# Who waits for the last two stores: moving one final wait from ScalarE to SyncE

## The chip, the cores and the metric

One core of one Trainium2 chip. The metric is device microseconds of one execution. The kernel takes about 98.8 us; its executions scatter by some 0.3 us.

## The reference, cut to what matters

One decoded token passes through attention over a window of 4096 keys and, in parallel, through an MLP. The result is one row of 1024 bfloat16 values.

```python
def reference(A_x, A_k_cache, A_v_cache, A_wq, A_wo, B_x, B_w1, B_b1, B_w2, B_b2):
    ...
    x = A_x                                       # 1 x 1 x 1024
    xn = _layernorm(x, axis=-1)
    return x + _A_ref(xn, A_k_cache, A_v_cache, A_wq, A_wo) + _B_ref(xn, B_w1, B_b1, B_w2, B_b2)
```

## The kernel before

Some 40 MB of weights and cache are loaded while the engines work behind the loads. The change touches only the end. TensorE collects the result in two halves of 512 columns, `ACC[0]` and `ACC[1]`. ScalarE copies the first half and SyncE stores it; VectorE copies the second and ScalarE stores that. Each storing engine then waits until its own store has landed.

```python
    with nc.body("pe_last", valid_engines=TENSOR):
        ...
        last.then_inc(s_fin, 1)
    ...
    dve.wait_ge(s_fin, 1)
    d_out = DVE.mark(dve.tensor_copy(OUT[32:33, :], ACC[1]))
    act.wait_ge(s_fin, 1)
    a_out = ACT.mark(act.activation(out=OUT[0:1, :], in_=ACC[0], func=ACTF.Copy))
    sp.wait_ge(ACT.sem, a_out)
    sp.dma_start(out_row[:, 0:512], OUT[0:1, :]).then_inc(s_out[0], 16)
    act.wait_ge(DVE.sem, d_out)
    act.dma_start(out_row[:, 512:1024], OUT[32:33, :]).then_inc(s_out[1], 16)
    sp.wait_ge(s_out[0], 16)
    act.wait_ge(s_out[1], 16)
```

Of the kernel before, what the change touches and what calls it, by code (L numbers as in the profile page):

```python
# [47 lines left out]
def bass_parallel_sum__sliding_block_cached__mixer_channel_mlp__decode_kernel(  # L48
# [21 lines left out]
    pe, dve, act, pool, sp = nc.tensor, nc.vector, nc.scalar, nc.gpsimd, nc.sync  # L70
# [12 lines left out]
    s_out = [nc.alloc_semaphore(f"s_out{n}") for n in range(2)]  # L83
# [490 lines left out]
    sp.dma_start(out_row[:, 0:512], OUT[0:1, :]).then_inc(s_out[0], 16)  # L574
    act.wait_ge(DVE.sem, d_out)
    act.dma_start(out_row[:, 512:1024], OUT[32:33, :]).then_inc(s_out[1], 16)
    sp.wait_ge(s_out[0], 16)
    act.wait_ge(s_out[1], 16)

    return nc  # L580

# [27 lines left out]
```

## Time and profile before

| | before |
|---|---|
| time, median of 3 runs | 98.78 us (98.54 to 98.88) |
| profiled run: time and span | 98.74 and 97.345 us |
| last matmul's semaphore to the end of the span | 1.977 us |

The span runs from the first to the last instruction that the profile records. The time is 1.4 us longer. No view shows it, but the trace's semaphore records go on past the span.

- **End**: the end of the span, which is the end of the last wait.
- **First barrier**: the nine steps of one semaphore that the kernel never names, counted in ns from the end. They are read as a barrier, in which each engine reports that it has arrived. A hop is the time from one step to the next; the turn is the hop from the fifth to the sixth. In the kernel before:

```
109  147  191  214  312  351  385  432     (the first of nine came at -1815)
```

- **Remainder**: time less span, averaged over the runs of a comparison. Spans are recorded to 0.1 us, so one run's remainder is coarse.

The rows of the profile that matter are shown in the prediction.

### The profile page before, as it was taken

What the parts mean: (1) busy time and instruction counts of PE and PEld (TensorE: products, weight loads), DVE (VectorE), ACT (ScalarE), POOL (GpSimd) and SP (SyncE); (2) the same over time, 40 slices, a digit from 0 to 9 for tenths busy, and PEclk for the clock granted to TensorE, in tenths of its full rate; (3) what the DMA queues carried; (4) which work ended last, traced back from release to release, by engine and by line L of the source; (5) the groups of instructions that cost most, each with busy time, mean ns of one, the idle gap of its engine ahead of it and who ended that gap; (6) DMA issues with size and microseconds to landing.
All of it is one profiled execution on the core that took longest, in us unless ns stands there. A gap on an engine that the chain in (4) does not pass through costs nothing.

```text
span 97.3 us, 1050 instructions
## 1 busy us (share of the span) xinstructions
PE 69.0 (71%) x330; PEld 32.3 (33%) x330; DVE 36.0 (37%) x49; ACT 5.8 (6%) x11; POOL 7.1 (7%) x23
## 2 busy tenths in 40 slices
PE   0001299999992139998999982169994699897881
PEld 0001154455550025655654431023341234332210
DVE  3705530000006999800999616794004300000002
ACT  0500060000000200000000000500000000000002
POOL 6796000000000000000000000000000000000000
PEclk9999999999999655999999999955699759999999
DMA  7999999989999989979999998888994999999970
GB/s 215 431 433 432 432 431 431 431 343 428 495 401 507 412 377 459 483 327 424 428 428 428 424 693 377 377 377 377 542 589 202 404 429 467 394 447 394 407 303 8
DMA packets 2773, 39.88 MB, mean 410 GB/s; under 512 B 322, under 2 KB 340, under 8 KB 724
## 3 DMA queue, kind: packets, MB, share of 16 engines
q1 hardware_dynamic: 2738, 39.85, 96.2%
q8 instruction: 1, 0.02, 0.1%
q10 hardware_dynamic: 34, 0.01, 0.1%
HBM read 39.86 MB, written 0.00 MB: 409 GB/s over the span
## 4 chain that ended last, share of the span: by engine, by line
DMA 79%; PE 15%; SPq 3%; issue 1%; DVE 1%; POOLq 0%
DMA W<-in_B_w_dram 42%; DMA KV<-in_A_wo_dram 37%; PE PS L404 7%; PE PS L388 7%; SPq L427 1%; SPq L169 1%; DVE KV L570 1%; SPq L179 0%; PE PS L560 0%; SPq L163 0%; POOLq L261 0%
## 5 line engine op out<-in xcount | busy, mean ns | idle before, releaser
L345 DVE STREAM_TRANSPOSE KV<-KV 128x4096 bf16<-128x4096 bf16 x4 | 17.5, 4424 | 5.3 <-DMA KV<-in_A_k_cache_dram 5.3
L388 PE MATMUL PS<-W,YZ 128*97 x64 | 14.7, 387 | 4.2 <-POOLq L261 4.1
L336 PE MATMUL PS<-WA,PT 128*97 x64 | 16.9, 434 | 0.2 <-issue 0.2
L388 PEld LDWEIGHTS PS<-W,YZ 128*97 x64 | 8.7, 136 | 10.2 <-issue 7.4
L336 PEld LDWEIGHTS PS<-WA,PT 128*97 x64 | 9.1, 142 | 7.7 <-issue 3.2
L505 PE MATMUL PS<-KV,PT 128*32 128x512 bf16 x32 | 9.8, 478 | 0.1
L538 PE MATMUL PS<-WA,GT 128*1 128x512 bf16 x56 | 7.9, 452 | 0.0
L570 DVE CAST KV<-PS 1x512 bf16<-1x512 f32 x1 | 0.7, 684 | 18.6 <-PE PS L560 18.6
L551 PE MATMUL PS<-W,OP 128*1 128x512 bf16 x48 | 6.8, 378 | 0.9 <-DMA W<-in_A_wo_dram 0.9
L296 PE MATMUL PS<-XT,meanf 128*128 128x16 f32 x2 | 0.6, 386 | 9.4 <-DVE XT L292 9.4
L348 DVE STREAM_TRANSPOSE TT<-PS 128x1024 f32<-128x1024 f32 x1 | 1.3, 1251 | 15.8 <-PE PS L336 15.8
L404 PE MATMUL PS<-KV,LQ 128*128 x32 | 7.1, 379 | 0.0
L505 PEld LDWEIGHTS PS<-KV,PT 128*32 128x32 bf16 x32 | 3.6, 116 | 5.8 <-issue 3.8
L404 PEld LDWEIGHTS PS<-KV,LQ 128*128 x32 | 3.1, 98 | 3.9 <-issue 0.6
L538 PEld LDWEIGHTS PS<-WA,GT 128*1 128x1 bf16 x56 | 2.7, 96 | 4.7 <-issue 2.3
L551 PEld LDWEIGHTS PS<-W,OP 128*1 128x1 bf16 x48 | 2.4, 83 | 5.3 <-DMA W<-in_A_wo_dram 1.2
L296 PEld LDWEIGHTS PS<-XT,meanf 128*128 128x128 f32 x2 | 0.5, 312 | 9.4 <-DVE XT L292 9.4
L510 DVE TENSOR_TENSOR TT<-PS,RM 32x512 f32<-32x512 f32 x1 | 0.7, 679 | 7.0 <-PE PS L505 7.0
L452 ACT ACTIVATE Pe<-PS,NMB 128x512 bf16<-128x512 f32 x2 | 1.3, 683 | 28.7 <-DVE NMB L449 28.7
L206 DVE MEMSET PS<- 128x3072 f32 x1 | 2.6, 2618 | 0.6 <-issue 0.6
L551 PE MATMUL PS<-KV,OP 128*1 128x512 bf16 x14 | 2.0, 378 | 0.6 <-DMA KV<-in_A_wo_dram 0.6
L431 DVE TENSOR_REDUCE MXP<-PS 128x1 f32<-128x1024 f32 x1 | 1.2, 1225 | 3.0 <-PE PS L404 3.0
(87 smaller groups left out, 30.1 us busy)
## 6 DMA issues: line engine op xcount, KB each, us to landing
WA<-in_A_wq_dram SPq DMA_DIRECT2D x2, 4096.0 KB, 16.7
W<-in_B_w_dram SPq DMA_DIRECT2D x2, 3584.0 KB, 37.1
WA<-in_B_w_dram SPq DMA_DIRECT2D x1, 7168.0 KB, 45.8
KV<-in_A_k_cache_dram SPq DMA_DIRECT2D x4, 1024.0 KB, 34.1
KV<-in_A_v_cache_dram SPq DMA_DIRECT2D x4, 1024.0 KB, 43.2
W<-in_A_wo_dram SPq DMA_DIRECT2D x1, 3840.0 KB, 33.5
W<-in_A_wo_dram SPq DMA_DIRECT2D x1, 2304.0 KB, 38.6
KV<-in_A_wo_dram SPq DMA_DIRECT2D x1, 1024.0 KB, 34.4
```

Source lines behind the costliest of these rows:

```text
L206: d_ps = DVE.mark(dve.memset(PS[:, 0:6 * 512], 0.0))
L336: last = pe.matmul(PS[0:97, n * 512:(n + 1) * 512], lhsT=shifted(XZ, s)[:, bass.ds(k, 1), :], rhs=wq_rows[:, bass.ds(k, 1), s * 1024 + n * ...
L345: dve.transpose(out=KT[:, g * W:(g + 1) * W], in_=KT[:, g * W:(g + 1) * W]).then_inc(r_k, 1)
L348: DVE.mark(dve.transpose(out=TT[:, :], in_=PS[:, 0:1024]))
L388: last = pe.matmul(PS[0:97, (2 + n) * 512:(2 + n) * 512 + HW], lhsT=shifted(YZ, s)[:, bass.ds(k, 1), :], rhs=w1_rows[:, bass.ds(k, 1), c: ...
L404: last = pe.matmul(PS[:, (4 + n) * 512:(5 + n) * 512], lhsT=q_blocks[:, bass.ds(g, 1), j, :], rhs=k_blocks[:, bass.ds(g, 1), n, :, j, :], ...
L431: d_mxp = DVE.mark(dve.tensor_reduce(out=MXP[:, 0:1], in_=PS[:, 4 * 512:6 * 512], axis=AX.X, op=ALU.max))
L452: a_exp = ACT.mark(act.activation(out=Pe[:, n * 512:(n + 1) * 512], in_=PS[:, (4 + n) * 512:(5 + n) * 512], func=ACTF.Exp, scale=SCALE, bi ...
L505: last = pe.matmul(PS[0:32, 0:512].rearrange("p (g d) -> p g d", g=HKV), lhsT=PT[:, b * 32:(b + 1) * 32], rhs=Vb[:, b, :, :], start=(b == ...
L538: pe.matmul(ACC[n], lhsT=GT[:, c:c + 1], rhs=W2[:, c * D + n * 512: c * D + (n + 1) * 512], start=False, stop=False)
L551: pe.matmul(ACC[n], lhsT=OP[:, r + u:r + u + 1], rhs=wo_at(r + u, 1)[:, n * 512:(n + 1) * 512], start=False, stop=False)
L570: d_out = DVE.mark(dve.tensor_copy(OUT[32:33, :], ACC[1]))
```

## The change

The intent: SyncE alone waits for both landings, so that ScalarE's program is over when it has issued its store.

```diff
     act.dma_start(out_row[:, 512:1024], OUT[32:33, :]).then_inc(s_out[1], 16)
-    sp.wait_ge(s_out[0], 16)
-    act.wait_ge(s_out[1], 16)
+    for s in s_out:
+        sp.wait_ge(s, 16)
```

## The prediction

> **What bounds the kernel now.** I began with the chain of work that ended last, since a change of the last two waits can only pay if those waits end the program.
>
> ```profile
> 59.33 0.04 issue
> 59.38 35.55 DMA KV<-in_A_wo_dram
> 94.92 0.04 issue
> 94.97 0.40 PE PS L560 x2
> 95.37 0.02 issue
> 95.39 0.68 DVE KV L570
> ```
>
> Columns: start, duration, what. Up to 94.92 us the kernel is a stream of loads; then two matmuls and one copy. The chain stops at 96.07 us (95.39 + 0.68) because waits are not counted as work, but the span is 97.3 us: the last 1.3 us, from the result's stores to the end, stand in no row of it. So I read the timeline of the end and then, line by line, the two final waits.
>
> ```profile
> 94.97 0.38 PE L560 MATMUL PS<-KV,OP 128*1 128x512 bf16 x2 [0.25 <-DMA KV<-in_A_wo_dram]
> 95.39 0.59 ACT L572 ACTIVATE KV<-PS 1x512 bf16<-1x512 f32 x1 [29.27 <-PE PS L560]
> 95.39 0.68 DVE L570 CAST KV<-PS 1x512 bf16<-1x512 f32 x1 [18.63 <-PE PS L560]
> 96.00 0.32 SPq L574 DMA_DIRECT2D out_dram<-KV  x1
> 96.11 0.25 ACTq L576 DMA_DIRECT2D out_dram<-KV  x1
> ```
>
> ```profile
> L577 SPq EVENT_SEMAPHORE  x1: 17/17/17, 97.1 to 97.1; - x1
> ```
>
> ```profile
> L578 ACTq EVENT_SEMAPHORE  x1: 17/17/17, 97.3 to 97.3; - x1
> ```
>
> The reader should see two parallel tails. ScalarE's copy is shorter, so SyncE issues its half first (96.00), waits, and passes at 97.1. VectorE's copy is longer, so ScalarE issues at 96.11 and passes its wait at 97.3. That wait is the last instruction of the span. The waiting itself appears only in the table of SyncE's waits:
>
> ```profile
> SPq L574 <- ACT KV L572: 36.2, 1, 36.2
> ...
> SPq L577 <- DMA out_dram<-KV: 0.8, 1, 0.8
> ```
>
> 0.8 us is the time from the end of SyncE's issue (96.00 + 0.32) to the landing. Finally the table by stretches of time, whose last two columns are the share of the DMA engines and GB/s:
>
> ```profile
> 96.50:96.70 0.20, 0.00 (x0) 0.00 (x0) 0.00 (x0) 0.00 (x0) 0.00 (x0) 1.00 0.29 82
> 96.70:96.90 0.20, 0.00 (x0) 0.00 (x0) 0.00 (x0) 0.00 (x0) 0.00 (x0) 1.00 0.03 10
> 96.90:97.10 0.20, 0.00 (x0) 0.00 (x0) 0.00 (x0) 0.00 (x0) 0.00 (x0) 1.00 0.00 0
> 97.10:97.34 0.24, 0.00 (x0) 0.00 (x0) 0.00 (x0) 0.00 (x0) 0.00 (x0) 0.61 0.00 0
> ```
>
> The packets are over by 96.90; the rest up to 97.3 is latency of the completion, with no engine at work. What the clock of the measurement adds lies outside the span: the profiled run took 98.74 us, 1.4 us more than 97.345 us. The trace holds semaphore updates there, after the last instruction, which I read next.
>
> **What the Trainium skill says.** "Perfetto Trace Analysis", Per-engine timelines: an instruction that only the sequencer executes is shown from the moment at which its semaphores are satisfied. Agrees: both waits show as 17 ns, starting some 20 ns after their semaphores' last updates (97.131 and 97.307 us in the trace's semaphore records).
>
> "DMA: Bandwidth & Descriptors", Latency and other measured facts: a tiny transfer can't go faster than some 800 ns. Agrees in size: SyncE's store landed 0.81 us after its issue ended, and 1.13 us after it began; ScalarE's 1.20 us after its issue began (97.307 - 96.108).
>
> "Runtime: NRT & Kernel Launch", The ~15µs preamble/postamble breakdown: behind the kernel stands a barrier of all engines[...], then a reset of semaphores, then another barrier. The trace agrees: one semaphore that the kernel never names is updated at 95.530, 97.454, 97.492, 97.536, 97.559, 97.657, 97.696, 97.730 and 97.777 us; then some 250 others are reset between 97.68 and 98.34; then the same semaphore steps nine times more, from 98.562 to 98.935. Hops are 23 to 47 ns, with one turn of 98 ns. The page gives no order of the engines, and this order is what decides here.
>
> **The change part by part.** It removes one 17 ns wait from ScalarE and adds the same wait to SyncE, behind SyncE's own. No store, copy, matmul, load or semaphore is touched.
>
> *To the end of the span.* SyncE's first wait passes at 97.148 and ends at 97.165. Its second finds its semaphore complete at 97.307, 0.14 us later, so it is already standing in that wait: it passes at about 97.33, as ScalarE did, and ends at 97.345. Two waits in series on events that come in this order cost the later event, not the sum. Effect: 0.00 us, at most 0.02 either way.
>
> *Behind the span.* This is the only place with something to win. The first barrier's updates read as a chain in which each engine adds one when its predecessor has: the first came at 95.530, 0.16 us after TensorE's last semaphore update (95.368), and no other engine had ended its work then, so first is TensorE. The second came at 97.454, 109 ns after ScalarE's end at 97.345; the third, fourth and fifth followed at hops of 38, 44 and 23 ns. An engine that had arrived before is passed at a hop's cost, so the one everybody waited for was the second, and ScalarE is the one that ended just before. That puts SyncE behind it; from the resets I take it for the fifth, since the highest block of semaphores (207 to 255) is the first to be reset, at 97.679, and the engine at the turn is the first to be free.
>
> With the change ScalarE ends at its issue's end, 96.361, and can step at about 96.36 + 0.11 = 96.47. The third and fourth, idle for long, follow by about 96.55. All three hops then lie under SyncE's wait. SyncE ends at 97.345 and steps some 0.10 us later (ScalarE's 109 ns, as an estimate), at 97.45 in place of 97.559. Everything after the turn follows as before.
>
> Sum: 38 + 44 + 23 = 105 ns off the path; +0.00 in the span; about -0.11 us altogether. From the median of 98.78 that gives 98.67 us, 0.1% less.
>
> **The rivals.** (1) *A full wait is saved*, because two engines waited and now one does: some 0.2 us (97.345 - 97.165). Against it: SyncE now waits for the same later event, and no earlier end is possible without an earlier landing. Would make 98.60 at most, and I give it little.
>
> (2) *Nothing at all moves.* The barrier's second step may have been held by something else. One thing speaks for this: the records of packets show one 16 KB instruction fetch from 96.511 to 97.439 us, 15 ns ahead of the step at 97.454. If it is the engine at that step which needs it, ScalarE's early end buys nothing: the chain still starts at 97.454, SyncE steps at 97.559, and the time stays 98.78. I can't tell from the records whose fetch it is. For ScalarE's wait speaks that the 109 ns are a reasonable time to leave a program, with TensorE's 162 ns beside it. The fetch could also start at another time once ScalarE runs on early.
>
> (3) *SyncE stands early in the chain, or is slow to leave its program.* Then the last to arrive has as many or more hops behind it than ScalarE had, and the time is up to 0.1 us longer: 98.8 to 98.9. Against it stands the order of the resets.
>
> (4) *ScalarE's early work behind its end disturbs the stores.* Its semaphore resets wait for the barrier, so nothing of it should meet the landing at 97.3. Worth 0.00.
>
> **Range and chances.** The expected step of 0.11 us is smaller than the scatter of the three runs before (98.54 to 98.88, 0.34 us). The range is therefore set by scatter: 98.45 to 98.92 around 98.67, with the upper part kept for rivals 2 and 3. A change of 2% is 1.98 us; that is more than the whole stretch from the start of the stores to the end of the span (97.345 - 96.003 = 1.34 us), so faster by it isn't to be had here, and slower would need a disturbance of the loads, which aren't touched. Chances: 0.01 faster, 0.98 within 2%, 0.01 slower.
>
> **What would show it.** In the changed kernel: ScalarE's last record is its store's issue, ending near 96.36; SyncE has two waits, the first passing at about 97.15, the second at about 97.33, both relative to stores issued at 96.00 and 96.11; the span stays 97.3 within the scatter of the loads. Behind it, the barrier's second, third and fourth steps lie before SyncE's end, and the fifth comes some 0.1 us after it, in place of 0.21 after the last instruction's end as now (97.559 - 97.345). If steps two to five still run in one row after SyncE's end, SyncE isn't the fifth (rival 3); if they come right behind an instruction fetch, it is rival 2. A time beyond 0.3 us from 98.78 with an unchanged tail would be the loads' scatter and say nothing of the change; a landing moved by over 0.1 us relative to its issue would break the first step.

## The result, and the profile after

The changed kernel took 98.56 us (median of 4 runs, 98.54 to 98.57), the kernel before 98.80 us (4 runs, 98.54 to 98.88). The ratio is 0.998, with a 95% interval of 0.9962 to 0.9998. A ratio here is the mean time of one kernel's runs over that of the other's of the same rounds, so not quite the ratio of the medians.

The timeline of the end, after the change (start, duration, engine, line, what):

```profile
94.92 0.38 PE L560 MATMUL PS<-KV,OP 128*1 128x512 bf16 x2 [0.25 <-DMA KV<-in_A_wo_dram]
95.34 0.59 ACT L572 ACTIVATE KV<-PS 1x512 bf16<-1x512 f32 x1 [29.26 <-PE PS L560]
95.34 0.68 DVE L570 CAST KV<-PS 1x512 bf16<-1x512 f32 x1 [18.53 <-PE PS L560]
95.95 0.32 SPq L574 DMA_DIRECT2D out_dram<-KV  x1
96.05 0.25 ACTq L576 DMA_DIRECT2D out_dram<-KV  x1
```

Every row starts some 0.05 us earlier than before, because the loads ended that much earlier in this execution. The distances are the same. The final wait, in the view of its source line:

```profile
L578 SPq EVENT_SEMAPHORE  x1: 28/28/28, 97.3 to 97.3; - x1
```

And SyncE's waits (us in total, times, longest):

```profile
SPq L574 <- ACT KV L572: 36.2, 1, 36.2
...
SPq L578 <- DMA out_dram<-KV: 1.0, 1, 1.0
```

There is one wait where the prediction expected two: the two conditions went into one instruction, of 28 ns in place of 17. SyncE now waits 1.0 us after its issue, not 0.8, since it waits for the later landing. The chain of work still ends as it did (start, duration, what):

```profile
59.33 35.54 DMA KV<-in_A_wo_dram
94.87 0.04 issue
94.92 0.40 PE PS L560 x2
95.31 0.02 issue
95.34 0.68 DVE KV L570
```

From the last matmul's semaphore to the end it is 1.981 us, against 1.977: nothing was won inside the span. Behind the end, the steps of the barrier's semaphore in ns (not a view of the profile; read from the trace's semaphore records):

```
before   -1815   109   147   191   214   312   351   385   432
after    -1819  -619  -580  -536   121   165   203   237   285
```

Three steps now lie before the end, and the ninth comes 147 ns sooner after it. The profiled executions differ by 0.17 us (98.74 and 98.57). That is 0.049 us of span, which is the loads, and 0.118 us from the end to the semaphore's last recorded step (1.590 and 1.472 us). The 0.147 us shrink to 0.118 because the very last hop of a second barrier took 91 ns instead of 62. Over 14 traces this hop was between 46 and 187 ns, in the same kernel too, so it is scatter.

### The profile page after: what moved, and what is told of

The parts are those of the page before. It is cut to its first block, busy times and chain, and to the rows that moved or that the text cites. A ratio compares the mean times of both kernels' runs of the same rounds, so it can differ in the third digit from the quotient of the medians.

```text
span 97.3 us, 1049 instructions
## 1 busy us (share of the span) xinstructions
PE 67.8 (70%) x330; PEld 31.7 (33%) x330; DVE 36.1 (37%) x49; ACT 5.8 (6%) x11; POOL 7.1 (7%) x23
## 4 chain that ended last, share of the span: by engine, by line
DMA 79%; PE 15%; SPq 3%; issue 1%; DVE 1%; POOLq 0%
DMA W<-in_B_w_dram 42%; DMA KV<-in_A_wo_dram 37%; PE PS L404 7%; PE PS L388 7%; SPq L427 1%; SPq L169 1%; DVE KV L570 1%; SPq L179 0%; PE PS L560 0%; SPq L163 0%; POOLq L261 0%
## 5 line engine op out<-in xcount | busy, mean ns | idle before, releaser
L336 PE MATMUL PS<-WA,PT 128*97 x64 | 15.6, 405 | 1.2 <-POOLq L261 1.1
L336 PEld LDWEIGHTS PS<-WA,PT 128*97 x64 | 8.4, 132 | 8.0 <-issue 3.7
```

The costliest lines, as they stand in the source:

```text
L336: last = pe.matmul(PS[0:97, n * 512:(n + 1) * 512], lhsT=shifted(XZ, s)[:, bass.ds(k, 1), :], rhs=wq_rows[:, bass.ds(k, 1), s * 1024 + n * ...
```

## The experiments

Theory A: the barrier is a chain in the order TensorE, ScalarE, GpSimd, VectorE, SyncE and back, and whoever arrives last has the hops behind it still to pay. The prediction had named only the first, second and fifth of these places; the third and fourth are first named in the expectations below. The main rivals: the gain comes from one wait less, or one instruction instead of two (D); it comes from an earlier instruction fetch (C). The first four kernels ran on one chip beside 11 runs of the kernel before, the next four on another beside 11, the last four on that second chip beside 12, of which 11 are the same ones.

### The changed kernel again, twice

No edit.

> The changed kernel once more, as the yardstick of this chip. 'Tail' below is the time from the end of the last instruction of the profile to the last update of the barrier's semaphore: 1.590 us in the kernel before, 1.472 us in the changed one. Theory A (the barrier behind the kernel is a chain TensorE, ScalarE, GpSimd, VectorE, SyncE; whoever comes last pays the hops that lie behind it): tail 1.47 +- 0.03, time 0.10 to 0.20 us under the kernel before. Rival B (the second 0.12 us of the 0.24 measured is a gain too): 0.24 us again. Rival C (the earlier instruction fetch, 95.96 in place of 96.51 us, is what helped): the fetch starts again near 96.0 and the tail goes with it.

> The changed kernel a third time, on another chip: its first comparison gave 0.24 us, its second nothing, with the loads ahead of the tail 0.14 us longer in that one. Theory A: first barrier 0.285, remainder 1.30 +- 0.04 beside 1.44 of before, and a time 0.15 +- 0.15 us under before, the spread being that of the loads.

Measured: 98.80 us against 98.78 (ratio 1.0002, 0.9988 to 1.0015), and 98.70 against 98.80 (0.9992, 0.9974 to 1.0009). The gain of 0.10 to 0.20 us expected of the first of them did not come. So neither comparison alone shows the gain in the time, and the 0.24 us of the first one doesn't repeat: rival B falls. The remainder shows it each time: 1.313 against 1.446 us, and 1.293 against 1.437. The barrier's ninth step came at 285 and 284 ns. The spans were longer instead, 97.50 against 97.36 us on average in the one and 97.42 against 97.34 in the other. Since the last matmul's semaphore to the end took 1.987 and 1.981 us in the traces, that difference lies ahead of the changed lines. Whether it is chance or belongs to this program isn't settled by six runs that scatter by 0.3 us.

The first four expectations speak of the "tail", up to the very last step. It came at 1.425 us here (a little under the 1.44 to 1.50 expected), at 1.440 with the waits crossed (under 1.47 to 1.53), at 1.618 with ScalarE waiting for both (inside) and at 1.595 with VectorE (over 1.52 to 1.58). It includes the last hop of 46 to 187 ns, so the later runs go by the first barrier instead.

### The kernel before as a control

No edit.

> The kernel before, unchanged, run as if it were a new one, to learn the noise of this comparison and to have a second trace of it. 'First barrier' below is the time from the end of the last instruction of the profile to the ninth step of the barrier's semaphore: 0.432 us in the kernel before and with ScalarE waiting for both, 0.285 in the changed kernel, 0.382 with VectorE waiting. 'Remainder' is the timed run less its span, averaged over the runs: 1.446 us before, 1.313 changed. Theory A: first barrier 0.432 again, remainder 1.40 to 1.50, ratio 1.000 +- 0.0015. Rival C (the instruction fetch belongs to the effect): the fetch starts 1.14 us after the last matmul's semaphore as in the first trace of before, where all the others have 0.64; if it is at 0.64 here too, it is chance and not part of the cause.

Measured: 98.83 against 98.81 us, ratio 1.0001 (0.9986 to 1.0017), first barrier 433 ns. The remainder was 1.492 us against 1.443 of the same kernel, so 0.05 us is the error of that measure. The tail was 1.788 us in this trace against 1.590 in the first one of the same kernel. The instruction fetch started 1.18 us after the last matmul's semaphore (1.14 in the first trace), so its late start seems to belong to this program. The next run tells whether it matters.

### One half of the change: SyncE waits for both, ScalarE keeps its wait

```diff
-    sp.wait_ge(s_out[0], 16)
+    for s in s_out:
+        sp.wait_ge(s, 16)
     act.wait_ge(s_out[1], 16)
```

> One half of the change alone: SyncE waits for both halves, but ScalarE keeps its own wait too, so both pass the same landing. Theory A: ScalarE is again among the last, its three hops come behind it: first barrier 0.432, remainder 1.44, no gain. If the gain came from SyncE's part (one instruction of two conditions, SyncE waiting longer), first barrier 0.285 and remainder 1.31.

```profile
L578 SPq EVENT_SEMAPHORE  x1: 28/28/28, 97.3 to 97.3; - x1
```

```profile
L579 ACTq EVENT_SEMAPHORE  x1: 17/17/17, 97.3 to 97.3; - x1
```

The two views of the last lines show both engines passing at the same landing. Measured: first barrier 424 ns, remainder 1.488 us, ratio 1.0015 (0.9997 to 1.0032). SyncE's part of the change gains nothing by itself; what counts is that ScalarE's wait is gone. The fetch started early here, 0.65 us after the last matmul's semaphore, with no gain from it: rival C falls. (The first barrier is 8 ns under 432 mainly because the end is SyncE's here, 7 ns after that of ScalarE's wait; counted from ScalarE's, the steps are those of the kernel before within 2 ns.) (The other half alone, no wait for the second store at all, could let the program end before its result has landed. It was not tried.)

### The waits crossed: ScalarE waits for SyncE's half, SyncE for ScalarE's

```diff
-    sp.wait_ge(s_out[0], 16)
-    act.wait_ge(s_out[1], 16)
+    act.wait_ge(s_out[0], 16)
+    sp.wait_ge(s_out[1], 16)
```

> ScalarE waits for SyncE's half (early, lands at about 97.1), SyncE for ScalarE's half (late, about 97.3): as many waits, on as many engines, as in the kernel before, only crossed. Theory A: what counts is that the last to arrive is SyncE. ScalarE steps at about 97.1 + 0.02 + 0.11 = 97.25, GpSimd at 97.29, VectorE at 97.33, all before SyncE at 97.42, so the tail is that of the changed kernel or a little more (1.47 to 1.53; the turn behind SyncE may cost more because VectorE stepped so lately), time 0.07 to 0.17 us under before. Rival D (it helps that ScalarE's program ends early, or that one wait fewer is made, or that two waits become one instruction): like before, tail 1.59.

```profile
L577 ACTq EVENT_SEMAPHORE  x1: 17/17/17, 97.4 to 97.4; - x1
```

```profile
L578 SPq EVENT_SEMAPHORE  x1: 17/17/17, 97.6 to 97.6; - x1
```

As many waits and instructions as before, only SyncE now passes last (97.6) and ScalarE first (97.4). The steps:

```
-1815   -64   -26    19   121   165   204   238   284
```

ScalarE, GpSimd and VectorE step around the end, SyncE 121 ns after it, and the ninth step comes at 284 ns, as in the changed kernel. The remainder is 1.287 against 1.446 us; the time 98.74 against 98.78, ratio 0.9988 (0.9973 to 1.0003). This separates A from D most clearly: nothing was removed, only the order of arrival was turned round, and the whole gain of the barrier is there.

### ScalarE alone waits for both

```diff
-    sp.wait_ge(s_out[0], 16)
-    act.wait_ge(s_out[1], 16)
+    for s in s_out:
+        act.wait_ge(s, 16)
```

> The mirror of the change: ScalarE alone waits for both halves, SyncE's program ends with its issue. Theory A: ScalarE is last in both this and the kernel before, so nothing changes: tail 1.59 +- 0.03, ratio to before 1.000 +- 0.002. Rival D (one engine waiting instead of two, one instruction instead of two, is the gain): tail about 1.47, 0.1 us or more under before.

Measured: first barrier 432 ns with every step behind the end within 1 ns of the kernel before, so one engine waiting instead of two is no gain. D falls from this side too. The ratio was 1.0013 (1.0000 to 1.0026), the remainder 1.536 against 1.446 us. That 0.09 us more is not in the barrier; it is about twice what the control showed of scatter. These are five runs whose remainders differ by 0.12 us (standard deviation), so it may be chance; no run settles it.

### VectorE, GpSimd or TensorE waits for both

Each is the same edit with `dve`, `pool` or `pe` in place of `act`.

> VectorE alone waits for both halves. Theory A: VectorE is the fourth of five, one hop (23 ns) ahead of SyncE, and its two steps must lie some 121 ns apart, as they did in the kernel before (97.536 and 97.657). Tail: 1.472 + 23 (SyncE's hop) + 54 (turn of 98 in place of 44 ns) = 1.55 us, with 0.03 either way for how quickly VectorE leaves its program; time between before and changed, some 0.04 us under before. If VectorE isn't the fourth but the third, 1.59. Rival D: 1.47.

> GpSimd alone waits for both. Theory A: it is the third of five, so two hops (44 and 23 ns) and the turn of 98 in place of 44 ns come behind it: first barrier 0.285 + 0.067 + 0.054 = 0.406 plus or minus 0.03 for how quickly GpSimd leaves. Remainder by that alone 1.43. VectorE's run had 1.63 where its barrier said 1.41; if an engine that does not store anything adds some 0.2 us behind the barrier (theory E), 1.6 to 1.65 here too; if that was VectorE's own, 1.43.

> TensorE alone waits for both halves. Theory A: it is the first of five, so all four hops (34, 38, 44, 23 ns) and the slow turn come behind it. It left its program 162 ns after its last semaphore where ScalarE took 109: first barrier 0.432 + 0.034 + 0.053 = 0.52 us, remainder 1.53, time 0.09 us over before. If the order were another (TensorE late in the chain), 0.30 to 0.45. GpSimd's run showed that an engine can take 0.54 us to leave; TensorE doing that too would give 0.9.

The steps of the barrier in ns after the end; a late first, third or fourth entry names the place of the engine that waits:

```
TensorE waits     186   220   259   303   326   424   462   498   545
ScalarE waits   -1832   109   147   191   214   312   350   386   432
GpSimd waits    -1819  -645   537   581   604   702   740   776   823
VectorE waits   -1823  -649  -611   140   164   261   299   335   382
SyncE waits     -1819  -619  -580  -536   121   165   203   237   285
```

This is the order of theory A, each place shown by delaying the engine in it. The prediction's sign for SyncE holds too: in all 14 traces the reset of the highest block of semaphores begins 118 to 131 ns after the fifth step, wherever that lies. Two further things can be read here. First, the step from the fifth to the sixth entry is 98 ns, but 44 where VectorE had stepped early: in the first four rows VectorE's two steps (fourth and sixth) lie 121 ns apart each time. When SyncE alone is late, that time has passed already. Second, the engines leave their programs at very different speed: 109 ns from the end for ScalarE, 121 for SyncE (110 in the run with one store), 140 for VectorE, 186 for TensorE and 537 for GpSimd. My expectation for GpSimd's first barrier (406 ns) failed on that alone; TensorE's (0.52 us against 545 ns) nearly held. The times and remainders expected of VectorE (some 0.04 us under before) and TensorE (remainder 1.53) failed, for reasons outside the first barrier.

| who waits for both | first barrier, ns | remainder, us | before's, us | ratio of times (95%) |
|---|---|---|---|---|
| SyncE (the change, second time) | 285 | 1.313 | 1.446 | 1.0002 (0.9988 to 1.0015) |
| VectorE | 382 | 1.630 | 1.446 | 1.0019 (1.0005 to 1.0033) |
| ScalarE | 432 | 1.536 | 1.446 | 1.0013 (1.0000 to 1.0026) |
| TensorE | 545 | 1.833 | 1.437 | 1.0048 (1.0029 to 1.0066) |
| GpSimd | 823 | 1.857 | 1.443 | 1.0040 (1.0024 to 1.0056) |

GpSimd's remainder is 0.41 us over before; its barrier says 0.39 (823 - 432). TensorE's is 0.40 over; its barrier says 0.11, and the time from the ninth step to the second barrier was 1034 ns instead of 785, 0.25 more, which I didn't expect and don't explain. The trace places it: the last reset came 559 ns after the ninth step (561 in the kernel before), and the second barrier began 475 ns after that instead of 224. The kernel before had 296 ns there in its other trace, so a part may be scatter. VectorE's is 0.18 over where its barrier says 0.05 under. The next run asks about that.

### The change, and VectorE waits for the early half as well

```diff
     for s in s_out:
         sp.wait_ge(s, 16)
+    dve.wait_ge(s_out[0], 16)
```

> The changed kernel, and VectorE waits besides for the half that lands early (some 0.18 us before the other). Its step then comes some 0.04 us ahead of SyncE's. Theory A: SyncE is still the last; first barrier 0.285 to 0.34 (the turn may cost up to 54 ns more as VectorE's two steps must lie 121 ns apart), remainder 1.30 to 1.37. With VectorE waiting for both the remainder was 1.63, 0.2 over what its barrier explains. Theory H (a wait at the end of VectorE's program costs 0.2 us outside the barrier, whether it is last or not): remainder 1.5 or more here too. If 1.3 to 1.4, that excess belongs to VectorE being the last.

```profile
L578 SPq EVENT_SEMAPHORE  x1: 28/28/28, 97.2 to 97.2; - x1
```

```profile
L579 DVEq EVENT_SEMAPHORE  x1: 21/21/21, 97.1 to 97.1; - x1
```

VectorE is not the last (97.1 before 97.2), the ninth step is at 285 ns as in the changed kernel, and yet the remainder is 1.540 us and the ratio 1.0010 (0.9995 to 1.0025). So a wait at the end of VectorE's program cost some 0.25 us here (1.540 - 1.293, the changed kernel on the same chip) outside the barrier, whether VectorE is last or not. In the two profiled executions with such a wait the time was 0.025 us under and 0.007 us over the semaphore's last step; in the other twelve it was 0.15 to 0.20 us under. The trace has nothing in which this could be seen, so what it is stays open.

### The issues exchanged

```diff
-    sp.wait_ge(ACT.sem, a_out)
-    sp.dma_start(out_row[:, 0:512], OUT[0:1, :]).then_inc(s_out[0], 16)
-    act.wait_ge(DVE.sem, d_out)
-    act.dma_start(out_row[:, 512:1024], OUT[32:33, :]).then_inc(s_out[1], 16)
+    act.wait_ge(ACT.sem, a_out)
+    act.dma_start(out_row[:, 0:512], OUT[0:1, :]).then_inc(s_out[0], 16)
+    sp.wait_ge(DVE.sem, d_out)
+    sp.dma_start(out_row[:, 512:1024], OUT[32:33, :]).then_inc(s_out[1], 16)
```

with the waits of the changed kernel.

> The change, and the two issues exchanged: ScalarE stores its own half when its copy is done, SyncE stores VectorE's half, then waits for both. From the traces SyncE's store lands 1.128 us after its issue begins, ScalarE's 1.199. ScalarE's half: issue at about 96.00, landing 97.20; SyncE's: issue at 96.10, landing 97.23, against 97.31 now. Theory F (an issue's cost goes with the engine that issues): last matmul's semaphore to the end of the span 1.90 in place of 1.98 us, first barrier 0.285, so 0.08 us better than the changed kernel. Rival G (the second issue of the two is slower whoever makes it, because both share something): 1.98 again.

```profile
95.98 0.25 ACTq L574 DMA_DIRECT2D out_dram<-KV  x1
96.08 0.32 SPq L576 DMA_DIRECT2D out_dram<-KV  x1
```

The first store landed at 97.097 us, 1.117 after its issue began; the second at 97.274, 1.198 after. The second store is slower by 0.07 to 0.08 us whoever issues it, and the last matmul's semaphore to the end took 1.977 us again: theory F missed, and the time is G's. But the same half is second in every run, so whether the order or the half makes it slower isn't separated. The packet records show where the difference lies: from the end of a store's last packet to its landing it is 0.330 us for the first and 0.398 us for the second (0.329 and 0.397 in the kernel before). The time was 98.57 against 98.81 us, ratio 0.9979 (0.9963 to 0.9995), with a remainder of 1.305 against 1.443 us. That is the change's own gain, with a luckier draw of the loads (span 97.28 us on average), not a better version.

### One store for both halves

```diff
     sp.wait_ge(ACT.sem, a_out)
-    sp.dma_start(out_row[:, 0:512], OUT[0:1, :]).then_inc(s_out[0], 16)
-    act.wait_ge(DVE.sem, d_out)
-    act.dma_start(out_row[:, 512:1024], OUT[32:33, :]).then_inc(s_out[1], 16)
+    sp.wait_ge(DVE.sem, d_out)
+    sp.dma_start(out_row.rearrange("o (n w) -> (o n) w", n=2), OUT[0:33:32, :]).then_inc(s_out[0], 16)
     sp.wait_ge(s_out[0], 16)
-    act.wait_ge(s_out[1], 16)
```

> One store of both halves, issued by SyncE when both copies are done, and one wait for it; ScalarE's program ends with its copy. From the traces: the second of two stores takes 1.20 us from issue to landing, the first 1.12, whoever issues. Theory I (the second store is slower because it comes behind the first): alone, issued at about 96.11 by the clock of the trace of before, it lands 1.13 us later, last matmul's semaphore to the end of the span 1.90 in place of 1.98 us, first barrier 0.285: 0.08 us under the changed kernel. Rival: two rows in one store cost what two stores do, 1.98.

```profile
96.06 0.61 SPq L575 DMA_DIRECT2D out_dram<-KV  x1
```

```profile
L576 SPq EVENT_SEMAPHORE  x1: 17/17/17, 97.7 to 97.7; - x1
```

A clear miss, of theory I and of its rival. The issue alone took 0.61 us instead of 0.32, its packets began 1.22 us after the issue's start instead of 0.75, and the landing came 1.59 to 1.62 us after its start (96.063 to 97.652 and 97.683). The last matmul's semaphore to the end rose to 2.453 us, the time to 99.08 against 98.80 us (ratio 1.0037, 1.0017 to 1.0057). Two stores on two engines were better here than one of two rows. No version tried here beats the change.

## Why the prediction was right or wrong

- **Where it could pay.** Right: the stretch up to the end of the span stayed 1.98 us, and what moved lies behind it.
- **The form of the wait.** Wrong in a detail: two waits in two records were expected and one of two conditions came. It changed the end by 11 ns of instruction at most.
- **The order of the barrier.** Right in the three places that it named (TensorE first, ScalarE second, SyncE fifth), and now shown by the delayed engines. In the prediction it was inferred from one trace, and one reason was misread: "no other engine had ended its work then" overlooks GpSimd, whose last record ends at 43.82 us.
- **Hops off the path.** The term of 38 + 44 + 23 = 105 ns is right; SyncE's time to leave was put at 0.10 us and measured 0.121.
- **The turn.** "Everything after the turn follows as before" is the sentence that failed. The turn itself fell from 98 to 44 ns. So the barrier gave 105 + 54 - 12 = 147 ns where 0.11 us was predicted.
- **The packets.** The 82 GB/s at 96.50 to 96.70 us are mostly the 16 KB instruction fetch, not the stores, whose own packets lie at 96.753 to 96.910 us. That they are over by some 96.9 us was right.
- **The rivals.** A full wait saved (1): no, the waits crossed show it. The fetch (2): it did move, from 96.51 to 95.96 us, but with half of the change it moved as well and nothing was gained. SyncE early in the chain (3): no. ScalarE's early end disturbing the stores (4): their landings after the issue are unchanged (1.126 and 1.197 us).
- **ScalarE's early step.** Expected at 96.47, it came at 96.677 us, 370 ns after its issue ended. That is off the path and cost nothing.
- **The number.** 98.67 was predicted, 98.56 measured, inside the range. That says little, since the range of 0.47 us was set by scatter and would have held "nothing moves" as well; the steps of the barrier are the evidence. The 0.24 us of the first comparison are more than the mechanism gives: the two later ones have -0.02 and 0.10 us between the medians. The remainders agree on 0.13 to 0.14 us, which is what the barrier says. The rest is the scatter of the loads, as the prediction had it.

## What to carry to other kernels

If several engines have something to wait for at the end, ask which of them stands last in the barrier behind the program, and give the latest wait to that one: here SyncE. With GpSimd, TensorE or VectorE waiting the remainder was 0.41, 0.40 and 0.18 us over that of the kernel before, so it pays to keep the last wait off these three here. The change is worth some 0.1 us, so take it only when it is free, and judge it by a measure that leaves the loads' scatter out, such as time less span and the steps of the barrier's semaphore.

## What the Trainium skill lacked or had wrong

- "Runtime: NRT & Kernel Launch", The ~15µs preamble/postamble breakdown: it doesn't give the order of the engines in the barrier. The runs show TensorE, ScalarE, GpSimd, VectorE, SyncE, and back for the first barrier behind the kernel. It gives 355 ns for eight hops of a barrier ahead of the kernel, and no hops for the one behind it. The one run that passes all eight behind the end (TensorE waiting: 186 to 545 ns) took 359 ns, and the same semaphore's last nine steps ahead of the kernel took 371 ns in the trace of before, but the hops aren't even: behind the end 34, 39, 44 and 23 ns up, then 98, and 38, 36 and 47 back. The 98 fell to 44 where VectorE had stepped early.
- Same section: it gives some 1.5 us for the reset of semaphores behind the kernel. In the kernel before the reset records run from 334 to 993 ns after the end, 0.66 us, and 785 ns passed from the end of the first barrier to the first step of the second (1217 - 432). That stretch was 783 to 787 ns in eleven of the 14 traces, 857 in the other trace of before, 885 with one store and 1034 with TensorE waiting.
- No page that I found says how long each engine takes from its last wait to its step in the barrier: 109 ns for ScalarE, 110 to 122 for SyncE, 140 for VectorE, 186 for TensorE, 537 for GpSimd.
- "DMA: Bandwidth & Descriptors", Latency and other measured facts: a floor of some 800 ns for a tiny transfer, which these runs don't contradict. It is only a lower bound: the 1 KB stores here landed some 1.13 us (first) and 1.20 us (second) after their issue began, and one store of two such rows 1.62 us, 0.61 us of it the issue.
